# Batch 0 of a cross-attention and ELU kernel: a new written-out order, with one conversion step per weight block on GpSimd

## The chip, the cores and the metric

The kernel runs on one NeuronCore of a Trainium2 chip. The metric is the device time of one execution in microseconds (us). A core has TensorE (PE in the profile) for matmuls, VectorE (DVE), ScalarE (ACT) and GpSimd (POOL) for elementwise work, and SyncE (SP), which here only issues DMA transfers. Each engine runs its own queue of instructions in order and waits on semaphores for the others. PSUM has eight banks of 128 x 512 float32; matmuls write there.

## What is computed

The input `x` is (8 batches, 8 heads, 512 tokens, 64), `state` is (8, 8, 32, 64). For each batch and head the tokens read from the states and the states from the tokens, by softmax attention; both results are concatenated to 544 rows of 512 columns per batch and go through a feed-forward layer with an ELU:

```python
scores = scale * np.matmul(x, state.transpose(0, 1, 3, 2))
a = softmax(scores)                      # over the 32 states
xread = np.matmul(a, state)
scores2 = scale * np.matmul(state, x.transpose(0, 1, 3, 2))
a2 = softmax(scores2)                    # over the 512 tokens
sread = np.matmul(a2, x)
out = np.concatenate([xread, sread], axis=2)
x = out.transpose(0, 2, 1, 3).reshape(B * S, H * D)     # 4352 x 512
h = x @ w_in                             # 512 x 2048
g = np.where(h > 0.0, h, np.exp(np.minimum(h, 0.0)) - 1.0)
return (g @ w_out).astype(np.float32)    # 2048 x 512
```

`x` and `state` are float32. `w_in` and `w_out` arrive as float64, so that the kernel reads 8 bytes for each weight and has to make a float32 of them by integer and float operations on their low and high 32-bit words.

## The kernel before

The tokens of a batch go through the layer as 16 slices of the hidden dimension (`fo`, 128 wide each). Since `xread` is a product with the states, the kernel doesn't form it: `make_m` multiplies the states by `w_in` once per batch (a product `m` for each 512 hidden columns `c`), and `ffn1` multiplies `m` by the turned softmax weights `aT`. `exp_part` and `max_part` form the ELU into `g_all`, and a second product with `w_out` gives the output. The rows that the states read are gathered in `read` and put through the layer at the end (`states`).

Batches 1 to 7 run in `batch`: all 16 slices of `ffn1`, then the second product in a Strassen form, with the attention of the next batch hooked between its steps. x of batches 2 to 7 comes a second time as 32 x 32 blocks (`load_blocks`), which VectorE turns (`turn_blocks`); their turned softmax weights are made by VectorE and transfers (`move_state`). In batch 1 VectorE also forms the weight sums for Strassen (`weight_sum`).

Batch 0 (`first_batch`) is different: the weights are still arriving. They are cut into 32 blocks of 128 x 512 weights (16 of `w_in`, four for each `c`; 16 of `w_out`, one for each `fo`). For each block a transfer loads the 512 KB of float64 (`load_weights`, tile `raw`), ScalarE makes three passes (`convert_1`: the low word scaled and shifted to a float, the same made a whole number, the absolute value of the high word), and VectorE makes four (`convert_2`: a clamp, a shift with a mask, a join with the sign bits, and the addition of the low part, which the profile calls CUSTOM_DVE_ANT_0). A few blocks (`NRAW` = 7) are in flight; each `convert_2` is followed by `fetch`, which issues the next load. After the last block `fetch` loads batch 1's x and writes the converted `w_in` to memory (`w_in_mem`), from where later batches bring it back.

The order of all of batch 0's work, and of batch 1's attention behind it, is written out by hand as the string `plan`. Each engine executes its own instructions in exactly this order (`InOrder`). The names in it:

- `kT`/`kTc`, `kU`/`kUc`: turn the states of batch 0, of the others, on PE and copy them out; `x:b.i`/`xc:b.i`: turn half of x on PE, copy it out; `sc`: the scores.
- Softmax of head group g: `tr` (32 x 32 turn), `tm` (maximum over states), `ps` (subtract, GpSimd), `te` (exp), `su` (sum), `pm` (scale, GpSimd), `tt` (turn to `aT`); for the state side `mx` (maximum), `ae` (exp), `sd` (reciprocal of the total), `sT`/`sTc` (turn on PE, copy), `sr`/`src` (`state_read`, `keep_read`).
- `w:k.1`, `w:k.2`: the two parts of the conversion of block k.
- `M:0.c.h`, `Mc`: half of `make_m`, its copy. `M:1.0` makes batch 1's first two products.
- `F:fo` is `ffn1`, `R:fo` is `exp_part`, `E:fo` is `max_part`, `O:fo` is `ffn2_row`, which adds slice `fo` to the four output banks 0 to 3.
- `Z:n`: n matmuls of the identity, which only keep PE busy.

F needs the turned weights `tt` and an `Mc` copy, which needs converted `w_in` blocks; O needs E and one converted `w_out` block.

Of the kernel before, what the change touches and what calls it, by code (L numbers as in the profile page):

```python
# [10 lines left out]
FP32 = mybir.dt.float32  # L11
# [14 lines left out]
def kernel(  # L26
# [61 lines left out]
    def pair(i):  # L88

        return psum[:, i : i + 2]  # L90
# [39 lines left out]

    x_t, st, m_t = {}, {}, {}

    def load_x(b, engines):
        x_t[b] = xpool.tile([P, R, DM], FP32, name="x_sb")
        x_v = x[b].rearrange("h (p r) d -> p r h d", r=R)
        for r in range(R):
            engines[r % len(engines)].dma_start(
                out=x_t[b][:, r].rearrange("p (h d) -> p h d", d=D), in_=x_v[:, r]
            )

    def load_blocks(b):

# [16 lines left out]
    def turn_blocks(b, m):  # L159

        i, j = divmod(m, 2)
        if j == 0:
            st[b, "xT", i] = work.tile([P, 2, R * P], FP32, tag="w", name="xT_b")
        st[b, m] = st[b, "xT", i][:, j]
        vector.transpose(st[b, m], st[b, "blocks", i][:, j])
# [18 lines left out]
        return raw  # L184

    def turn_states(raw, b0, b1):
        ps = st["k_ps"] = pair(6)[:, :, : (b1 - b0) * 64].rearrange("p t (b q) -> p t b q", q=64)
        for b in range(b1 - b0):
            transpose(ps[:, :, b], raw[:, b].rearrange("p c d -> p (c d)"))

# [14 lines left out]
    def high_words(raw):  # L205
        return raw.bitcast(U32).rearrange("p n (j w) -> p n j w", w=2)[:, :, :, 1]

    def convert_1(dst, raw):

        lo, hi = low_words(raw), high_words(raw)

        scalar.activation(
            out=lo.bitcast(FP32), in_=lo, func=AF.Copy, scale=2.0**-29, bias=2.0**23
        )
        scalar.activation(out=lo, in_=lo.bitcast(FP32), func=AF.Copy, bias=-(2.0**23))


        scalar.activation(out=dst, in_=hi.bitcast(FP32), func=AF.Abs)  # L220

    def convert_2(dst, raw):
        lo, hi = low_words(raw), high_words(raw)
        vector.tensor_scalar(
            out=dst, in0=dst, scalar1=as_float(896 << 20),
            scalar2=as_float((1151 << 20) - 1), op0=ALU.max, op1=ALU.min,
        )

        bits = dst.bitcast(U32)
        vector.tensor_scalar(  # L230
            out=bits, in0=bits, scalar1=3, scalar2=0x3FFFFFF8,
            op0=ALU.logical_shift_left, op1=ALU.bitwise_and,
        )
        vector.scalar_tensor_tensor(
            out=bits, in0=hi, scalar=0xC0000000, in1=bits,
            op0=ALU.bitwise_and, op1=ALU.bitwise_or,
        )
        vector.tensor_tensor(out=bits, in0=bits, in1=lo, op=ALU.add)
# [18 lines left out]
                transpose(ps[:, :, j, r], x_t[b][:, r, m * P : (m + 1) * P])  # L257
        st[b, "xT", i] = ps

    def copy_x(b, i):  # L260
        xT = opool.tile([P, 2, R * P], FP32, tag="o", name="xT")
        for j in range(2):
            st[b, 2 * i + j] = xT[:, j]
            scalar.copy(
                out=xT[:, j].rearrange("p (r t q) -> p t r q", t=2, q=64),
                in_=st[b, "xT", i][:, :, j],
            )

    def by_state(b, rhs, first=6):

# [147 lines left out]
    def make_m(b, c, h=None, first=6):  # L418

        c_in = c if b < 2 else c % 2  # L420
        halves = slice(2 * c_in, 2 * c_in + 2) if h is None else slice(2 * c_in + h, 2 * c_in + h + 1)
        assert h is None or b == 0
        st[b, "m", c] = by_state(b, [w_in[:, halves, m] for m in range(NP)], first)

    def copy_m(b, c, g, copy):
        if g == 0:
            m_t[b, c] = mpool.tile([P, G, 512], FP32, name="m_sb")
        copy(out=m_t[b, c][:, g], in_=st[b, "m", c][:, g])

    def copy_half(b, c, h):  # L430
        if h == 0:
            m_t[b, c] = mpool.tile([P, G, 512], FP32, name="m_sb")
        scalar.copy(
            out=m_t[b, c][:, :, h * 256 : (h + 1) * 256], in_=st[b, "m", c][:, :, :256]
        )

    def exp_part(ps):
# [301 lines left out]
    def first_batch():  # L739
# [4 lines left out]

        plan = """
            kT kTc x:0.0 xc:0.0 x:0.1 w:0.1 xc:0.1 w:0.2 w:1.1 sc:0 Z:14 tr:0.0 tr:0.1 w:2.1 tm:0.0
            tm:0.1 ps:0.0 w:3.1 mx:0.1 mx:0.0 ps:0.1 w:1.2 ae:0.0 te:0.1 ae:0.1 sd:0.0 su:0.1 w:5.1
            M:0.0.0 sd:0.1 pm:0.1 w:3.2 Mc:0.0.0 te:0.0 sT:0 w:4.1 tt:0.1 su:0.0 sTc:0 w:5.2 pm:0.0  # L750
            w:8.1 Z:8 sr:0 tt:0.0 src:0 w:2.2 Z:14 F:0 w:6.1 F:1 w:8.2 R:0 M:0.0.1 R:1 E:0 Mc:0.0.1
            E:1 O:0 w:9.1 w:4.2 w:10.1 w:9.2 F:2 w:7.1 w:6.2 M:0.1.0 F:3 R:2 w:7.2 Mc:0.1.0 O:1
            w:11.1 E:2 R:3 w:10.2 M:0.1.1 w:12.1 F:4 w:11.2 Mc:0.1.1 O:2 R:4 E:3 w:14.1 w:12.2 F:5
            w:13.1 E:4 w:14.2 O:3 R:5 w:16.1 E:5 w:13.2 F:6 w:17.1 w:16.2 M:0.2.0 R:6 F:7 w:18.1
            w:17.2 O:4 Mc:0.2.0 w:18.2 w:20.1 kU w:15.1 E:6 O:5 w:20.2 w:21.1 w:15.2 w:19.1 F:8 kUc
            O:6 R:8 w:21.2 R:7 w:22.1 E:7 M:0.2.1 E:8 F:9 w:19.2 Mc:0.2.1 w:23.1 M:0.3.0 F:10 w:22.2
            w:24.1 O:7 w:23.2 R:9 Mc:0.3.0 E:9 w:25.1 w:24.2 M:0.3.1 F:11 Mc:0.3.1 R:10 w:25.2 O:8
            R:11 E:10 w:26.1 E:11 F:12 w:29.1 w:26.2 O:9 w:30.1 w:29.2 w:27.1 F:13 w:30.2 w:28.1
            O:10 w:27.2 R:13 R:12 w:28.2 x:1.0 w:31.1 O:11 E:12 E:13 xc:1.0 w:31.2 x:1.1 O:12 xc:1.1
            sc:1 O:13 mx:1.1 mx:1.0 ae:1.1 tr:1.0 ae:1.0 tr:1.1 sd:1.0 sT:1 tm:1.0 tm:1.1 ps:1.0  # L760
            F:14 sTc:1 sd:1.1 ps:1.1 te:1.0 sr:1 R:14 su:1.0 F:15 te:1.1 pm:1.0 E:14 src:1 su:1.1
            O:14 R:15 tt:1.0 pm:1.1 E:15 tt:1.1 M:1.0 O:15 Mc:1.0
        """.split()
        make_identity(nc, ident)
        o_ps = [bank(c) for c in range(R)]
        order = [lambda k=k: load_w_in(0, k) for k in range(4)]
        for c in range(1, FC + 1):
            if c < FC:
                order += [lambda c=c, k=k: load_w_in(c, k) for k in range(4)]
            order += [lambda fo=fo: load_w_out(fo) for fo in range(4 * c - 4, 4 * c)]  # L770
        w, h, e = [], {}, {}

        def fetch():
            if len(w) == 12 and len(raw_states) == 1:
                raw_states.append(load_states(1, B))
            if len(w) < len(order):
                w.append(order[len(w)]())
            elif 1 not in x_t:
                load_x(1, [sync])
                for c in range(FC):  # L780
                    k = slice(2 * c, 2 * c + 2)
                    sync.dma_start(out=w_in_mem[:, k], in_=w_in[:, k])

        raw_states = [load_states(0, 1, [sync, scalar])]
        load_x(0, [sync, scalar])
        for k in range(NRAW):
            fetch()
        groups = {
# [8 lines left out]
        for step in plan:  # L797
# [5 lines left out]
                copy_states(*((0, 1) if name == "kTc" else (1, B)))  # L803
            elif name == "Z":
                for i in range(num[0]):
                    matmul(bank(3)[:, :P], ident, ident, start=True, stop=True)
            elif name in groups:
                groups[name](*num)
            elif name in whole:
                whole[name](*num)  # L810
            elif name == "w":
                (convert_1, convert_2)[num[1] - 1](*w[num[0]])
                if num[1] == 2:
                    fetch()
            elif name == "F":
                h[num[0]] = ffn1(0, num[0])
            elif name == "R":
                e[num[0]] = exp_part(h[num[0]])
            elif name == "E":
                max_part(num[0], e[num[0]], h[num[0]])  # L820
            elif name == "O":
                ffn2_row(o_ps, num[0])
            elif name == "x":
                turn_x(*num)
            elif name == "M":
                make_m(*num)
                if len(num) == 2:
                    make_m(1, 1, first=4)
            elif name == "xc":
                copy_x(*num)  # L830
            else:
                assert name == "Mc", step
                if len(num) == 3:
                    copy_half(*num)
                else:
                    for g in range(G):
                        copy_m(*num, g, scalar.copy)
        for g in range(G):
            copy_m(1, 1, g, scalar.copy)

# [6 lines left out]
    def batch(b):  # L847
        if b + 1 < B:
            load_blocks(b + 1)
        for fo in range(FO):  # L850
            elu(ffn1(b, fo), fo)
            if fo > 11 and b + 1 < B:
                turn_blocks(b + 1, fo - 12)
            if fo == FO // 4 + 1:
                for c in (2, 3):
                    make_m(b, c, first=6 if c == 2 else 0)
            if FO // 4 + 1 <= fo < FO // 4 + 5:
                c, g = divmod(fo - FO // 4 - 1, G)
                copy_m(b, 2 + c, g, vector.tensor_copy)
# [50 lines left out]
                )  # L910

    first_batch()
    load_x(2, [sync])
    for e in (scalar, gpsimd):
        e.on = False
    for b in range(1, B):
# [32 lines left out]
```

## Time and profile before

| quantity | value |
|---|---|
| time, median of three runs | 747.63 us (746.75 to 747.82) |
| span of the profiled execution | 744.4 us, 11377 instructions |
| PE busy | 723.7 us (97%) |
| VectorE busy | 486.0 us (65%) |
| ScalarE busy | 293.3 us (39%) |
| GpSimd busy | 34.4 us (5%), 38 instructions |
| first F of batch 0 starts | 31.96 us |
| last O of batch 0 ends, first F of batch 1 starts | 128.7 us |
| conversion of the last weight block ends | 105.5 us |

The profile gives the time of one execution from its first to its last instruction. Busy time of PE is not PE at its peak: matmuls are pipelined and their ends are modelled, so the spacing of their starts says more than their lengths. In the views of the trace a row begins with the start and the length in us, then the engine, the line (all instructions issued through `InOrder` have line 100), the operation, the tile written and the tile read, the shapes, the count of instructions merged into the row, and in brackets how long the engine had been idle and who released it.

### The profile page before, as it was taken

To read this page: it belongs to the slowest core of one execution; us is meant where nothing else is said; L and a number is where in the kernel's file an instruction comes from. 1 tells how busy PE (TensorE), PEld (TensorE's weight loads), DVE (VectorE), ACT (ScalarE), POOL (GpSimd) and SP (SyncE) were. 2 spreads that over 40 slices of the span, in tenths; PEclk is the share of its full clock that TensorE was granted. 3 is DMA by queue.
4 is the path that set the end of the run, shared out by engine and by line. 5 is a ranking of instruction groups with operands and counts; after the bars stand their busy time and mean duration, and the time that the engine had idled before them with its cause. 6 is when DMAs were issued, how large, how long until landed. Compare 5 with 4: busy or idle time off the path is not lost.

```text
span 744.4 us, 11377 instructions
## 1 busy us (share of the span) xinstructions
PE 723.7 (97%) x4472; PEld 502.5 (68%) x4472; DVE 486.0 (65%) x892; ACT 293.3 (39%) x539; POOL 34.4 (5%) x38
## 2 busy tenths in 40 slices
PE   4899999989999999999999999999999999999998
PEld 2544444348874798469944896479746894699886
DVE  2999975799437883677556864787367845556231
ACT  5899955542126311651055203621264106400420
POOL 0100002002000200010000200020002000000000
PEclk9999999999999999999999999999999999999999
DMA  9667900801634063503461164307340403003000
GB/s 282 225 201 239 326 0 1 167 4 22 177 94 133 5 179 84 160 1 106 122 153 46 26 173 110 116 13 187 83 144 1 143 33 137 1 1 142 29 4 25
DMA packets 126366, 76.25 MB, mean 102 GB/s; under 512 B 113768, under 2 KB 114280, under 8 KB 122472
## 3 DMA queue, kind: packets, MB, share of 16 engines
q1 hardware_dynamic: 124004, 74.90, 34.8%
q10 hardware_dynamic: 2308, 0.62, 0.4%
q8 instruction: 35, 0.57, 0.3%
q14 instruction: 19, 0.16, 0.1%
HBM read 59.24 MB, written 13.11 MB: 97 GB/s over the span
## 4 chain that ended last, share of the span: by engine, by line
PE 89%; DVE 6%; SPq 1%; DMA 1%; ACT 1%; issue 1%; POOL 0%; ACTq 0%; DVEq 0%; POOLq 0%
PE ps L100 89%; DVE w_in L100 2%; SPq L100 1%; DMA x_sb<-in_x_dram 1%; DVE g_all L100 1%; DVE total_t L100 0%; DVE s L100 0%; DVE top L100 0%; DVE w_out L100 0%; ACT e_sb L100 0%; POOL t_sb L100 0%; ACT xT L100 0%; DVE xT_b L100 0%; DVE aT L100 0%; DVE t_sb L100 0%
## 5 line engine op out<-in xcount | busy, mean ns | idle before, releaser
L100 PE MATMUL ps<-w_out,g_all 128*128 128x256 f32 (+2 forms) x1088 | 232.5, 366 | 1.1 <-DVE g_all L100 0.8
L100 PE MATMUL ps<-aT,m_sb 128*128 128x512 f32 x512 | 226.3, 595 | 1.1 <-DVE m_sb L100 0.8
L100 PEld LDWEIGHTS ps<-w_out,g_all 128*128 128x128 f32 x1088 | 176.6, 191 | 53.5 <-issue 37.1
L100 PEld LDWEIGHTS ps<-aT,m_sb 128*128 128x128 f32 x512 | 95.4, 190 | 122.0 <-issue 109.1
L100 ACT ACTIVATE e_sb<-ps 128x512 f32<-128x512 f32 (+1 forms) x144 | 82.5, 573 | 220.4 <-PE ps L100 205.1
L100 DVE SCALAR_TENSOR_TENSOR g_all<-e_sb,ps 128x512 f32<-128x512 f32 (+1 forms) x144 | 94.2, 656 | 101.0 <-ACT e_sb L100 100.4
L100 DVE TENSOR_TENSOR o_sb<-o_sb,ps 128x128 f32<-128x128 f32 (+2 forms) x170 | 52.6, 310 | 75.2 <-PE ps L100 73.5
L100 ACT ACTIVATE e_sb<-e_sb 128x512 f32<-128x512 f32 (+1 forms) x144 | 87.3, 606 | 4.6
L100 PE MATMUL ps<-t_w,s 128*128 128x256 f32 (+1 forms) x480 | 88.8, 339 | 0.0
L100 PEld LDWEIGHTS ps<-t_w,s 128*128 128x128 f32 x480 | 77.6, 191 | 8.1 <-DVE o_sb L100 0.2
L100 ACT COPY o_sb<-ps 128x512 f32<-128x512 f32 (+2 forms) x52 | 20.6, 424 | 151.7 <-PE ps L100 144.6
L100 ACT ACTIVATE raw<-raw 128x512 f32<-128x512 uint32 x64 | 43.7, 683 | 1.0
L100 DVE TENSOR_TENSOR s<-s,g_all 128x512 f32<-128x512 f32 (+1 forms) x36 | 32.2, 897 | 15.9 <-PE ps L100 15.5
L100 POOL TENSOR_TENSOR t_sb<-t_sb,top_t 128x512 f32<-128x512 f32 x16 | 16.7, 1047 | 517.0 <-DVE top_t L100 517.0
L100 DVE TENSOR_TENSOR g_all<-g_all,s 128x512 f32<-128x512 f32 (+1 forms) x36 | 32.1, 891 | 9.6 <-PE ps L100 9.6
L100 PE MATMUL ps<-w_in,kT 64*32 64x512 f32 (+1 forms) x576 | 34.0, 547 | 0.9 <-ACT a_s L100 0.9
L100 DVE TENSOR_TENSOR g_all<-g_all 128x512 f32<-128x512 f32 (+1 forms) x36 | 32.2, 894 | 0.5
L100 DVE TENSOR_TENSOR s<-g_all 128x512 f32<-128x512 f32 (+1 forms) x36 | 31.6, 883 | 0.8 <-DMA aT_s<-a_blocks 0.4
L100 PE MATMUL ps<-t_w,g_all 128*128 128x128 f32 (+1 forms) x240 | 32.1, 282 | 0.0
L100 PE MATMUL ps<-w_in,s 128*128 128x128 f32 x240 | 31.2, 277 | 0.0
L100 PEld LDWEIGHTS ps<-t_w,g_all 128*128 128x128 f32 x240 | 29.8, 192 | 0.5
L100 PEld LDWEIGHTS ps<-w_in,s 128*128 128x128 f32 x240 | 28.7, 192 | 0.6 <-DVE o_sb L100 0.5
(86 smaller groups left out, 557.1 us busy)
## 6 DMA issues: line engine op xcount, KB each, us to landing
w_in<-w_in_mem SPq DMA_DIRECT2D x26, 1024.0 KB, 5.9
raw<-in_moe_w_in_dram SPq DMA_DIRECT2D x16, 512.0 KB, 4.6
raw<-in_moe_w_out_dram SPq DMA_DIRECT2D x16, 512.0 KB, 4.5
out_dram<-o_sb SPq DMA_DIRECT2D x16, 512.0 KB, 2.8
x_sb<-in_x_dram SPq DMA_DIRECT2D x30, 256.0 KB, 4.9
x_blocks<-in_x_dram SPq DMA_DIRECT2D x96, 64.0 KB, 2.4
w_in_mem<-w_in SPq DMA_DIRECT2D x4, 1024.0 KB, 8.3
aT_s<-a_blocks SPq DMA_DIRECT2D x96, 32.0 KB, 1.9
```

Source lines behind the costliest of these rows:

```text
L100: ins = getattr(self.engine, name)(*args, **kw)
```

## The change

The conversion is cut into smaller steps, and one of them goes to GpSimd for each block. For even blocks (`held`) it is the clamp (`hold`), which VectorE did; for odd blocks it is the second pass on the low word (`whole_low`), which ScalarE did. So VectorE has three passes for even blocks and four for odd ones, ScalarE three and two. In the plan `w:k.1` is ScalarE's part, `w:k.0` GpSimd's and `w:k.2` VectorE's.

The plan of batch 0 is new. x of batch 0 is loaded in two halves of the heads, and each turned half is copied by ScalarE (`xc`) and VectorE (`xd`) together. `w_out` blocks are loaded right after the four `w_in` blocks of the same `c`. Two conversions instead of five stand ahead of the first F on VectorE; the states of the other batches are turned early (`kU`); the third and fourth M are made whole. Batch 1's x is now loaded as blocks and turned by VectorE (`bt`), and its state weights are turned by `move_state` (`ab`) like those of the later batches; the read of its states moves into `batch(1)` after slice 5, with the load of batch 2's x. The save of `w_in` to memory is issued after the plan. Some PSUM banks change to fit.

```diff
-    def load_x(b, engines):
+    def load_x(b, engines, parts=1):
         x_t[b] = xpool.tile([P, R, DM], FP32, name="x_sb")
         x_v = x[b].rearrange("h (p r) d -> p r h d", r=R)
...
+        n = H // parts
+        for i in range(parts):
+            for r in range(R):
+                engines[r % len(engines)].dma_start(
+                    out=x_t[b][:, r, i * n * D : (i + 1) * n * D].rearrange(
+                        "p (h d) -> p h d", d=D
+                    ),
+                    in_=x_v[:, r, i * n : (i + 1) * n],
+                )
...
-        ps = st["k_ps"] = pair(6)[:, :, : (b1 - b0) * 64].rearrange("p t (b q) -> p t b q", q=64)
+        ps = st["k_ps"] = pair(2 if b0 else 6)[:, :, : (b1 - b0) * 64].rearrange("p t (b q) -> p t b q", q=64)
...
+    def whole_low(raw, engine):
+        lo = low_words(raw)
+        if engine is scalar:
+            scalar.activation(out=lo, in_=lo.bitcast(FP32), func=AF.Copy, bias=-(2.0**23))
+        else:
+            engine.tensor_scalar(
+                out=lo, in0=lo.bitcast(FP32), scalar1=-(2.0**23), scalar2=None, op0=ALU.add
+            )
...
+    def hold(dst, engine):
+
+        engine.tensor_scalar(
             out=dst, in0=dst, scalar1=as_float(896 << 20),
             scalar2=as_float((1151 << 20) - 1), op0=ALU.max, op1=ALU.min,
         )
...
         plan = """
...
+            kT kTc x:0.0 xc:0.0 xd:0.0 x:0.1 xd:0.1 xc:0.1 sc:0 w:0.1 tr:0.1 tr:0.0 w:1.1 w:0.0
+            tm:0.1 tm:0.0 mx:0.1 w:1.0 w:2.1 mx:0.0 w:0.2 ps:0.1 ae:0.1 w:1.2 ae:0.0 ps:0.0 te:0.1
+            Z:26 sT:0 w:2.0 te:0.0 kU sTc:0 su:0.1 M:0.0.0 w:3.1 su:0.0 pm:0.1 sr:0 kUc pm:0.0 w:4.1
+            tt:0.1 w:3.0 tt:0.0 Mc:0.0.0 w:2.2 w:5.1 Z:8 F:0 w:4.0 w:6.1 w:3.2 F:1 w:5.0 R:0 sd:0.1
+            M:0.0.1 w:4.2 w:6.0 Mc:0.0.1 w:7.1 E:0 R:1 w:7.0 w:5.2 O:0 w:8.1 E:1 w:7.2 w:10.1 w:8.0
...
+            w:27.2 w:29.1 F:11 w:30.1 w:29.0 E:10 M:0.3 w:28.2 O:10 R:11 w:30.0 w:29.2 Mc:0.3 w:31.1
+            F:12 E:11 w:31.0 w:30.2 O:11 R:12 bt:1.2 w:31.2 F:13 E:12 bt:1.1 O:12 R:13 bt:1.0 bt:1.3
+            E:13 sc:1 F:14 mx:1.0 tr:1.0 ae:1.0 mx:1.1 O:13 R:14 sd:1.0 tm:1.0 ae:1.1 E:14 ps:1.0
+            sd:1.1 ab:1 te:1.0 F:15 su:1.0 O:14 R:15 tr:1.1 pm:1.0 tm:1.1 tt:1.0 ps:1.1 E:15 te:1.1
+            M:1.0 su:1.1 pm:1.1 O:15 Mc:1.0 tt:1.1
         """.split()
+        held = range(0, 32, 2)
...
+        order = []
+        for c in range(FC):
+            order += [lambda c=c, k=k: load_w_in(c, k) for k in range(4)]
+            order += [lambda fo=fo: load_w_out(fo) for fo in range(4 * c, 4 * c + 4)]
...
             elif 1 not in x_t:
+                load_blocks(1)
                 load_x(1, [sync])
...
-        load_x(0, [sync, scalar])
+        load_x(0, [sync, scalar], 2)
...
+                if step == 0:
+                    hold(dst, gpsimd) if holds else whole_low(raw, gpsimd)
+                elif step == 1:
+                    low_part(raw)
+                    if holds:
+                        whole_low(raw, scalar)
+                    high_part(dst, raw)
+                else:
+                    if not holds:
+                        hold(dst, vector)
+                    join(dst, raw)
                     fetch()
...
+        for c in range(FC):
+            k = slice(2 * c, 2 * c + 2)
+            sync.dma_start(out=w_in_mem[:, k], in_=w_in[:, k])
...
+                if b == 1:
+                    state_read(1)
+                    keep_read(1)
+                    load_x(2, [sync])
                 for c in (2, 3):
-                    make_m(b, c, first=6 if c == 2 else 0)
+                    make_m(b, c, first=0 if (c == 2) == (b == 1) else 6)
...
     first_batch()
-    load_x(2, [sync])
```

## The prediction

> **What bounds the kernel now.** I read the page's shares first: TensorE (PE) is busy 97% of the span, so only stretches in which it stands or starts late can be won. The chain of waits says where those are. Its columns are start, length (us) and what was waited for:
>
> ```profile
> 2.37 6.56 DMA x_sb<-in_x_dram
> ...
> 31.29 0.62 DVE aT L100
> ...
> 36.40 0.61 DVE g_all L100
> 37.05 102.14 PE ps L100 x470
> ```
>
> Before 37 us the chain goes through the load of x, then VectorE (DVE), and after it through PE alone to 139 us. So the start belongs to DMA, ScalarE and VectorE. The windows view (busy us and instruction count of each engine per stretch) shows how close the others come afterwards:
>
> ```profile
> 32.00:37.00 5.00, 4.26 (x24) 1.58 (x24) 4.79 (x10) 2.50 (x5) 0.00 (x0) 1.00 0.86 290
> 37.00:60.00 23.00, 22.95 (x82) 9.80 (x83) 22.07 (x41) 21.48 (x37) 0.00 (x0) 1.00 0.65 200
> 60.00:100.00 40.00, 40.00 (x163) 16.78 (x162) 38.13 (x70) 37.61 (x64) 0.00 (x0) 1.00 0.73 242
> 100.00:128.70 28.70, 28.70 (x203) 12.67 (x202) 15.87 (x34) 13.55 (x28) 4.15 (x4) 1.00 0.00 1
> ```
>
> After the time columns stand PE, PE weight loads, VectorE, ScalarE and GpSimd. From 37 to 100 us PE is full, but VectorE is at 95% and ScalarE at 94%: the conversion of the weights only just keeps up. GpSimd does nothing there. Whatever brings PE forward must bring VectorE forward too. The timeline prices the work on PE:
>
> ```profile
> 95.89 1.88 PE L100 MATMUL ps<-aT,m_sb 128*128 128x512 f32 x4
> 97.60 3.60 PE L100 MATMUL ps<-w_out,g_all 128*128 128x512 f32 x8
> 101.13 0.71 PE L100 MATMUL ps<-ident,x_sb 64*128 64x64 f32 x16
> 101.77 3.70 PE L100 MATMUL ps<-w_out,g_all 128*128 128x512 f32 x8
> ```
>
> By the starts, an F (two matmuls of `ffn1`) after another costs 1.71 us, an O (`ffn2_row`) 3.5, half of x's turn 0.65. Batch 0's last O ends and batch 1's first F starts at 128.72.
>
> **What the Trainium skill says.** "SBUF — State Buffer", section "Who interferes with whom": VectorE and GpSimd share one pair of SBUF ports under an exclusive lock; a VectorE instruction in a two-port mode (`tensor_scalar`, copies), or with two SBUF inputs against a GpSimd instruction that reads SBUF, blocks fully until the other is done. The trace agrees:
>
> ```profile
> 28.27 1.56 DVE L100 TENSOR_SCALAR w_in<-w_in 128x512 f32<-128x512 f32 x2
> 28.50 1.05 POOL L100 TENSOR_TENSOR t_sb<-t_sb,total_t 128x512 f32<-128x512 f32 x1 [3.57 <-DVE total_t L100]
> ...
> 91.58 0.69 DVE L100 SCALAR_TENSOR_TENSOR w_out<-raw,w_out 128x512 uint32<-128x512 uint32 x1
> 92.30 0.69 DVE L100 CUSTOM_DVE_ANT_0 w_out<-raw,w_out 128x1024 uint16<-128x1024 uint16 x1
> 92.91 0.88 DVE L100 TENSOR_SCALAR w_out<-w_out 128x512 f32<-128x512 f32 x2
> 93.83 0.69 DVE L100 SCALAR_TENSOR_TENSOR w_out<-raw,w_out 128x512 uint32<-128x512 uint32 x1
> ...
> 176.62 1.05 POOL L100 TENSOR_TENSOR t_sb<-t_sb,total_t 128x512 f32<-128x512 f32 x1 [1.69 <-DVE total_t L100]
> 176.98 1.24 DVE L100 TENSOR_TENSOR t<-t_w,t 128x512 f32<-128x512 f32 x1
> ```
>
> Two `tensor_scalar` take 0.88 us alone (92.91) and 1.56 when GpSimd runs at 28.50. The two-input instruction at 176.98 takes 1.24 where its like in batch 1 takes 0.68: GpSimd ends at 177.67, and it ends 0.55 later. So a blocked instruction is shortened by about 0.13 [...], and one GpSimd instruction of length p put between two such VectorE ones costs VectorE p - 0.13. All instructions of a conversion on VectorE are of these two kinds; only `max_part`, which reads PSUM and one SBUF tile, and some of the softmax are free of it.
>
> **The start.** x comes in halves of four transfers. They landed at 5.9, 7.1, 8.3 and 8.9 us by PE's starts; the first half, half of the bytes, should be there by 6.4. Its turn (0.8) and its two copies, now one each on ScalarE and VectorE at 0.55 rather than two in a row, lie beside the second half's landing. That lands at about 9 (more issues, same bytes); turn 0.9, copies 0.6: scores at 10.65 instead of 13.72. VectorE starts on them 2.1 later (15.84 before): 12.8. Then two `tr` 1.3, two `tm` 1.25, two `mx` 1.55: 16.9. Then only two conversions stand ahead of the first F, not five: 1.81 (blocks whose clamp is on GpSimd: one block's 2.25, from the starts 91.58 and 93.83, less 0.44) and 2.25, with 0.5 lost to GpSimd: 21.5. Sums 1.8, the other states' copy 1.1, two turns 1.3: first F at 25.8 instead of 31.96, so 6.2 earlier. The loads of the other states now come ahead of raw block 4; ScalarE is not there before 20, so I cost it nothing.
>
> **What PE needs from there.** 16 F and 16 O: 16 x (1.72 + 3.43) = 82.4; M: one half 0.6, two halves 1.2, two whole 1.95; scores 1.1; batch 1's first M 1.95: 89.2 in all, so 115.0 if nothing stands in its way. Gone are x's turn (1.4) and the turn of batch 1's weights (1.0), whose work goes to VectorE and transfers; the read of batch 1's states (1.1) moves into batch 1; the turn of the states (0.65) now lies in the start.
>
> **What VectorE needs.** After the first F, 30 blocks are left: 15 x 1.81 + 15 x 2.25 = 60.9. Twelve `max_part` at 0.60: 7.2; two small totals and the first turn of batch 1's blocks: 1.15. Sum 69.2, so the last conversion would end at 95.0 without GpSimd. After it come E:12 (0.6) and then PE's remainder, whose order leaves no second gap: four O, two F, scores and M, 20.2. End is the last conversion + 20.8: 115.8, level with PE's bound.
>
> To this comes the lock. GpSimd has about 28 instructions in the stretch. No row shows a one-input instruction on it at this size. Upper bound: its two-input row at 28.50, 1.05 us. Lower: "GPSIMD Engine Reference", section 3.1, gives 1.03 cycles an element for at most two operations, an estimate of 0.44 us for 512 at 1.2 GHz; the same section measures 0.77 for 512 elements in a longer loop. Its section 7 has a penalty for steps above 8 bytes; the low words lie exactly 8 apart, so I take none. No run here shows any of these. I take 0.50, nearer the low end because both steps have one input and one or two operations. Cost: 28 x (0.50 - 0.13) = 10.4. `max_part` and the small work make up 12% of VectorE's time, and a waiting GpSimd instruction slips into them; I say a quarter is hidden: 7.8. The last conversion ends at 102.8, the batch at 123.6, against 128.7: 5.1 won.
>
> ScalarE isn't the bound: three instructions for 15 blocks at 1.87, two for 14 at 1.25, R at 1.2 and the copies of M are about 64 us in these 77. What waits behind a late join on VectorE is the next E, and behind that an O on PE; that is the sum's assumption.
>
> **Batch 1.** It gains 1.1 on PE and 0.5 on ScalarE. In the chain, VectorE carries the work from 140.5 to 146.3 and from 157 to 166.2, with PE standing 0.8 and 2.3 us ahead of those ends. So most of the 1.1 hides; I add 0.5. The save of `w_in` (4 MB, 8.3 us to landing each) now goes right before batch 0's stores and the x blocks of batch 2. Those blocks were issued by 148.2 and first turned at 156.3, so some 5 us of delay are hidden. Later batches are untouched. Together 747.6 - 5.1 + 0.5 = **743.0**.
>
> **Rivals.** (1) GpSimd's work slips almost wholly into gaps of VectorE: PE's 115.0 sets the end, 13.7 won, 0.5 given back: 734.4. For it: ScalarE and GpSimd steps are placed some slots ahead of each join. Against it: VectorE has few gaps. (2) GpSimd is slow, and the lock becomes the bound. At 0.77 the lock costs 28 x 0.64 x 0.75 = 13.4, the batch ends at 129.2, 748.6 in all; at 1.05, 28 x 0.92 x 0.75 = 19.3, it ends at 135.1, and the time is 754.5: slower. With nothing hidden, 761. For it: VectorE was already 95% busy, so each wait lands on the path. Against it: one input, not two. (3) The start is won but batch 1 gives it back, since VectorE bounds it and the late transfers meet it: about 747.
>
> **Chances.** Forecast 0.45 (0.40 of it faster, the rest near nothing or beyond, since p decides), hidden 0.15, slow GpSimd 0.30, given back 0.10 (0.04 faster, 0.04 same, 0.02 slower). Faster 0.59, same 0.07, slower 0.34. The range goes from the hidden case to a little beyond the slow one, leaving out the unhidden 761: 734 to 757.
>
> **What would show it.** First `ps<-aT,m_sb` near 26 us; scores near 10.7; GpSimd rows of 0.5 us for `raw` and `w_in`/`w_out`; VectorE's 0.69 us rows in the conversion lengthened on average, by 5 to 10 us in the stretch; last conversion near 103; batch 1's first F near 123.6. A GpSimd row of 0.8 or more, or PE waiting long on VectorE between 40 and 100 us, would make it wrong on the slow side; lengths that stay at 0.69 on the fast side.

## The result, and the profile after

The changed kernel takes 754.93 us (median of 4 runs, 754.59 to 756.5), the kernel before in the same comparison 747.73: a ratio of 1.0103, 95% interval 1.0085 to 1.012. It is slower by 7.2 us, where 743.0 and a gain were forecast. The span of the profiled execution grew from 744.4 to 752.9 us, by 8.5.

The chain of waits of the changed kernel, to be held against the one before (start, length, what was waited for):

```profile
26.85 0.65 DVE aT L100
...
30.67 1.05 DVE w_in L100
...
110.53 0.69 DVE g_all L100
111.27 35.86 PE ps L100 x212
```

VectorE is now on the chain until 111 us, where before PE carried it from 37 us. The first F did start earlier (27.65 instead of 31.96 us), but the lead was then lost. The windows of the changed kernel (after the time columns PE, PE weight loads, VectorE, ScalarE, GpSimd, then the granted PE clock, the DMA share and GB/s) show the new bound:

```profile
27.00:60.00 33.00, 29.29 (x102) 11.90 (x103) 31.08 (x52) 23.08 (x42) 24.22 (x13) 0.90 0.61 199
60.00:111.00 51.00, 46.79 (x131) 18.42 (x129) 47.93 (x76) 34.39 (x59) 29.65 (x17) 1.00 0.51 124
111.00:132.00 21.00, 20.73 (x89) 8.38 (x90) 13.17 (x29) 8.57 (x18) 4.19 (x4) 1.00 0.14 23
```

PE, full before from 37 to 100 us, now has holes; VectorE is busy 94% of 27 to 111 us. ScalarE has been relieved (from 94% of 37 to 100 us before to 68% here), which won no time. GpSimd works 53.9 us of these 84. Its groups (count, then busy us and mean ns of one, then idle time) give the price that the prediction had to guess:

```profile
L100 POOL TENSOR_SCALAR raw<-raw 128x512 uint32<-128x512 f32 x16 | 26.9, 1687 | 4.6 <-ACT raw L100 3.7
L100 POOL TENSOR_SCALAR w_in<-w_in 128x512 f32<-128x512 f32 x8 | 17.2, 2157 | 18.1 <-ACT w_in L100 16.1 <-DVE w_in L100 1.3 <-DMA raw<-in_moe_w_in_dram 0.6
L100 POOL TENSOR_SCALAR w_out<-w_out 128x512 f32<-128x512 f32 x8 | 15.9, 1988 | 11.5 <-ACT w_out L100 11.2
```

A low-word pass takes 1.69 us and a clamp 2.0 to 2.2, not 0.50. A clamp takes VectorE 0.42. How the two engines meet is seen in the timeline of the changed kernel:

```profile
47.65 1.96 POOL L100 TENSOR_SCALAR w_out<-w_out 128x512 f32<-128x512 f32 x1 [3.91 <-ACT w_out L100]
47.85 0.96 DVE L100 CUSTOM_DVE_ANT_0 w_in<-raw,w_in 128x1024 uint16<-128x1024 uint16 x1
48.73 0.41 DVE L100 TENSOR_SCALAR w_in<-w_in 128x512 uint32<-128x512 uint32 x1
49.18 0.69 DVE L100 SCALAR_TENSOR_TENSOR w_in<-raw,w_in 128x512 uint32<-128x512 uint32 x1
49.68 1.69 POOL L100 TENSOR_SCALAR raw<-raw 128x512 uint32<-128x512 f32 x1
49.90 1.09 DVE L100 CUSTOM_DVE_ANT_0 w_in<-raw,w_in 128x1024 uint16<-128x1024 uint16 x1
```

While the clamp runs from 47.65 to 49.61, one VectorE instruction is lengthened (0.96 instead of 0.69) and the next two keep their usual 0.41 and 0.69, though both are of the kinds that were expected to wait. Then the low-word pass adds 0.40 to the next one (1.09). So GpSimd's instructions are much longer than assumed, but take only a part of their length from VectorE.

VectorE's row of work from 27.43 us to the end of the last conversion at 109.16 has no gap over 0.14 us: 81.7 us for 30 blocks. By the rates of before it is 69.2 as predicted, and 0.6 for one weight sum that got in between: 11.9 are lost, 0.42 for each of 28 GpSimd instructions.

A second loss lies in batch 1. From its first F to the start of the last part of batch 2's scores pass 40.3 us (131.83 to 172.12) instead of 37.5 (128.72 to 166.23). VectorE's timeline says why; first the kernel before, from the third turn of batch 2's blocks to the fourth:

```profile
160.28 0.70 DVE L100 STREAM_TRANSPOSE xT_b<-x_blocks 128x512 f32<-128x512 f32 x1
...
164.87 0.68 DVE L100 TENSOR_TENSOR t<-t_w,t 128x512 f32<-128x512 f32 x1
165.47 0.70 DVE L100 STREAM_TRANSPOSE xT_b<-x_blocks 128x512 f32<-128x512 f32 x1
```

Then the changed kernel, up to the third turn:

```profile
163.76 0.68 DVE L100 TENSOR_TENSOR t<-t_w,t 128x512 f32<-128x512 f32 x1
...
165.49 0.69 DVE L100 TENSOR_TENSOR t<-t_w,t 128x512 f32<-128x512 f32 x1
166.09 0.69 DVE L100 TENSOR_TENSOR t_w<-t_w 128x512 f32<-128x512 f32 x1
166.70 0.69 DVE L100 TENSOR_TENSOR w_out<-w_out 128x512 f32<-128x512 f32 x1
167.30 0.68 DVE L100 TENSOR_TENSOR w_in<-w_out 128x512 f32<-128x512 f32 x1
167.90 0.70 DVE L100 STREAM_TRANSPOSE xT_b<-x_blocks 128x512 f32<-128x512 f32 x1
```

Five weight sums for the second level of Strassen (`second[k].weights`) stand ahead of the last two turns of batch 2's blocks; in the kernel before there was one between them. No line of the diff moves them. They are issued after `vector.on = False`, where the compiler of the program may choose the place, and with another order in front of them it chose another one. Three more such sums stand in batch 0, two of them right behind the last conversion and ahead of E:12; these stood there in the kernel before too (at 105.48 and 106.21 us), and the forecast left them out. PE waits 1.28 and 2.41 us for the turns; its granted clock falls to 0.82 from 172 to 180 us, and the last scores and the first M products there, 2.7 us long before (166.23 to 168.93), take 4.0 (172.12 to 176.15).

Three parts of the 8.5 us between the two spans are thus placed: 3.1 at the end of batch 0 (131.83 against 128.72), 2.8 in batch 1 and 1.3 behind it. The last 1.3 arise in the later batches. Batch 3, from first F to first F, lasts 80.8 instead of 79.7 us; it lasts 80.5 to 81.0 in every trace of the new order below and 79.7 to 79.8 in every one of the old. The cause of this stays open.

### The profile page after: what moved, and what is told of

It is laid out like the page before. It is cut to its first block, busy times and chain, and to the rows that moved or that the text cites. A ratio compares the mean times of both kernels' runs of the same rounds, so it can differ in the third digit from the quotient of the medians.

```text
span 752.9 us, 11333 instructions
## 1 busy us (share of the span) xinstructions
PE 728.7 (97%) x4396; PEld 501.0 (67%) x4396; DVE 494.5 (66%) x884; ACT 278.7 (37%) x515; POOL 94.3 (13%) x70
## 4 chain that ended last, share of the span: by engine, by line
PE 78%; DVE 13%; DMA 3%; SPq 2%; issue 2%; ACT 1%; POOL 0%; DVEq 0%; POOLq 0%
PE ps L100 78%; DVE w_in L100 4%; DVE w_out L100 4%; SPq L100 2%; DVE g_all L100 1%; DMA raw<-in_moe_w_in_dram 1%; DVE s L100 1%; DMA x_sb<-in_x_dram 1%; DMA aT_s<-a_blocks 1%; ACT e_sb L100 0%; DMA s_first<-in_state_dram 0%; DVE m_sb L100 0%; DVE total_t L100 0%; DVE top L100 0%; DVE xT_b L100 0%
## 5 line engine op out<-in xcount | busy, mean ns | idle before, releaser
L100 PE MATMUL ps<-w_out,g_all 128*128 128x256 f32 (+2 forms) x1088 | 236.1, 369 | 6.1 <-DVE g_all L100 2.5
L100 PEld LDWEIGHTS ps<-w_out,g_all 128*128 128x128 f32 x1088 | 177.3, 192 | 63.7 <-issue 36.8
L100 DVE SCALAR_TENSOR_TENSOR g_all<-e_sb,ps 128x512 f32<-128x512 f32 (+1 forms) x144 | 94.3, 655 | 100.7 <-ACT e_sb L100 100.2
L100 PE MATMUL ps<-w_in,kT 64*32 64x512 f32 (+1 forms) x544 | 36.4, 587 | 3.7 <-DVE w_in L100 3.0
L100 ACT ACTIVATE raw<-raw 128x512 f32<-128x512 uint32 (+1 forms) x48 | 32.5, 677 | 0.5
```

The source lines that it names most:

```text
L100: ins = getattr(self.engine, name)(*args, **kw)
```

## Experiments

Theory A: GpSimd's steps cost VectorE more through the shared ports than they take off it. Theory B: the new order itself lost the time, by its start, by PE's clock or in batch 1. Theory C, for batch 1: the sums that moved ahead; its rival D: the late transfers. The table gives the time of each run, the ratio to the kernel before in the same comparison, and from its profile the start of the first F, the end of the last conversion, the start of batch 1's first F, and the us from there to the start of the last part of batch 2's scores.

| run | time | ratio (95%) | first F | last conversion | batch 1's F | batch 1 |
|---|---|---|---|---|---|---|
| before | 747.7 | | 31.96 | 105.5 | 128.7 | 37.5 |
| changed | 754.9 | 1.0103 (1.0085 to 1.012) | 27.65 | 109.2 | 131.8 | 40.3 |
| e1_no_gpsimd | 747.2 | 0.9989 (0.9981 to 0.9997) | 26.16 | 102.3 | 123.5 | 40.3 |
| e2_clamp_only | 747.2 | 0.9992 (0.9982 to 1.0001) | 26.09 | 100.8 | 123.5 | 40.3 |
| e3_weights_after_turns | 750.0 | 1.0029 (1.002 to 1.0038) | 27.81 | 107.8 | 129.2 | 37.4 |
| e4_before_spare_clamp | 757.8 | 1.0123 (1.0101 to 1.0144) | 34.36 | 116.3 | 139.6 | 37.5 |
| e5_no_gpsimd_late | 743.8 | 0.9939 (0.9924 to 0.9954) | 26.64 | 102.3 | 123.5 | 37.4 |
| e6_clamp_only_late | 742.1 | 0.9916 (0.9901 to 0.9931) | 26.61 | 100.7 | 122.4 | 37.4 |
| e7_before_late | 746.6 | 0.9975 (0.9965 to 0.9986) | 32.23 | 105.7 | 129.0 | 36.2 |
| e8_low_only | 756.5 | 1.0105 (1.009 to 1.012) | 26.34 | 111.8 | 133.0 | 40.3 |
| e9_before_spare_low | 761.8 | 1.0198 (1.0178 to 1.0218) | 33.82 | 118.7 | 142.1 | 37.5 |
| e10_before_spare_low_dense | 759.4 | 1.0165 (1.0146 to 1.0184) | 34.88 | 117.4 | 140.6 | 37.5 |
| e11_x_whole | 743.2 | 0.9947 (0.9931 to 0.9964) | 27.47 | 101.9 | 123.3 | 37.4 |
| e12_all_clamps_late | 742.5 | 0.9942 (0.9925 to 0.996) | 28.07 | 101.1 | 123.2 | 37.4 |

### No GpSimd step, and only one kind of it

```diff
-                if step == 0:
-                    hold(dst, gpsimd) if holds else whole_low(raw, gpsimd)
-                elif step == 1:
+                if step == 1:
                     low_part(raw)
-                    if holds:
-                        whole_low(raw, scalar)
+                    whole_low(raw, scalar)
                     high_part(dst, raw)
-                else:
-                    if not holds:
-                        hold(dst, vector)
+                elif step == 2:
+                    hold(dst, vector)
                     join(dst, raw)
```

> The changed kernel with no conversion step on GpSimd: the clamp of even blocks back on VectorE (ahead of the join), the low word's second pass of odd blocks back on ScalarE; order otherwise that of the change. Theory A (GpSimd's steps of 1.6 to 2 us cost VectorE more through the shared ports than the clamps they take off it): in the profile of the changed kernel VectorE needs 81.8 us from 27.4 to 109.2 for work that is 69.9 at the rates of before, 11.9 lost to some 28 GpSimd steps, 0.42 each; the 15 clamps that come back cost 15 x 0.44 = 6.6. So the last conversion should end some 5 us earlier, near 104, batch 1's first F near 126, and the time be about 749. Theory B (the new order itself, not GpSimd, is what lost: PE's slow clock from 33 to 42 us, the start, batch 1): VectorE and ScalarE only get more to do, and the time is 755 to 762.

Measured: 747.2 us, and batch 1's first F 8.3 us earlier than in the changed kernel. VectorE has 15 clamps more in the stretch and is done 6.9 us sooner. That is more than the 749 and the 126 of the expectation. Theory A holds, and for batch 0 B falls: the new order without GpSimd gains 5.2 us up to the end of batch 0. Batch 1 and what lies behind it take nearly all of it back, so for batch 1 B stands; the runs with late sums below take it up.

e2 keeps the clamps of even blocks on GpSimd, e8 the low-word passes of odd blocks:

```diff
                 if step == 0:
-                    hold(dst, gpsimd) if holds else whole_low(raw, gpsimd)
+                    if holds:                          # e2
+                        hold(dst, gpsimd)
...
+                    if not holds:                      # e8
+                        whole_low(raw, gpsimd)
```

> The changed kernel with only the clamps of even blocks on GpSimd (16 instructions of 1.95 us); the low word's second pass of odd blocks is back on ScalarE. Theory A: half of the lost 11.9 us goes, VectorE's own work stays as in the changed kernel: last conversion near 103, time about 749, the same as with no GpSimd step, since a clamp costs 0.42 through the ports and saves 0.44. If the longer clamp costs more than the low-word pass, it is slower than the run with no GpSimd step, 751 or more. Theory B: ScalarE only gets more to do, time 755 or more.

> The changed kernel with only the low word's second pass of odd blocks on GpSimd, the clamps all on VectorE. By differences, 16 clamps on GpSimd changed nothing (first F of batch 1 at 123.5 with and without), so the 16 low-word passes must carry the 8.3 us, about 0.5 each though they are the shorter ones (1.65 against 1.95 us). Expected: first F of batch 1 at 131 to 132, time 754 to 756. If the two kinds only hurt together (GpSimd's queue too full), 748 to 750.

Measured: with the clamps 747.2 us, where 749 was expected, and batch 1's first F at 123.5 as without GpSimd. That these agree is in part chance: VectorE's last conversion ends 1.5 us sooner with the clamps on GpSimd, but two weight sums (1.3 us) follow it there, which in e1 stand further back. With the low-word passes 756.5, first F at 133.0, some 1 us beyond what was expected. The summed length of VectorE's conversion instructions tells the two kinds apart: it is 71.4 us without GpSimd, 69.4 with 16 clamps there, 78.6 with 16 low-word passes. A clamp saves VectorE 0.42 and gives back (69.4 - 71.4 + 16 x 0.42) / 16 = 0.29 of it; a low-word pass saves VectorE nothing and costs (78.6 - 71.4) / 16 = 0.45. It was taken off ScalarE, which had time. So e2 and e8 part what A had put into one price: the low-word passes are the loss, the clamps are not.

### The ports alone

The kernel before gets one GpSimd instruction per block on a spare tile that nobody reads: e4 a clamp, e9 the low-word pass at steps of 8 bytes, e10 the same on adjacent elements.

```diff
                 (convert_1, convert_2)[num[1] - 1](*w[num[0]])
+                if num[1] == 1:
+                    gpsimd.tensor_scalar(
+                        out=spare, in0=spare, scalar1=as_float(896 << 20),
+                        scalar2=as_float((1151 << 20) - 1), op0=ALU.max, op1=ALU.min,
+                    )
```

> The kernel before, with one extra GpSimd clamp of 128 x 512 on a spare tile for each of the 32 blocks, placed after ScalarE's part in the order; nothing reads the tile, so no engine waits for it and only the shared ports can cost time. Theory A (0.42 us of VectorE for each): VectorE, 95% busy in batch 0, needs 32 x 0.42 = 13 us more, and the time is 755 to 760. If a GpSimd step held the ports for all of its 1.95 us: 50 us more, 785 or above. If the cost in the changed kernel is the chain (joins that wait for the slow GpSimd step) and not the ports: 747 to 749.

> The kernel before with one extra GpSimd low-word pass (float read and uint32 written, both at steps of 8 bytes, 512 elements) on a spare tile for each of the 32 blocks; nothing reads it. If the ports alone make the low-word pass dear (0.5 to 0.6 us of VectorE each by the difference of the runs with and without it), VectorE loses 16 to 19 us and the time is 762 to 767, clearly above the 757.8 of the spare clamps. If in the changed kernel it was the chain (VectorE's clamp and join waiting for a slow pass), the spare pass costs no more than the spare clamp: 756 to 759.

> As the run before, but the spare pass reads and writes 512 adjacent elements. If the 8-byte steps make the pass hold the ports longer, this costs clearly less than the strided one, as much as a spare clamp or less: 755 to 759. If the kind of operation does (one operand, float to uint32), it costs the same as the strided one.

The groups of GpSimd in e4, e9 and e10, one fence for each:

```profile
L100 POOL TENSOR_SCALAR t<-t 128x512 f32<-128x512 f32 x32 | 63.7, 1990 | 2.3
```

```profile
L100 POOL TENSOR_SCALAR t<-t 128x512 uint32<-128x512 f32 x32 | 53.5, 1671 | 2.3
```

```profile
L100 POOL TENSOR_SCALAR t<-t 128x512 uint32<-128x512 f32 x32 | 50.3, 1572 | 2.3
```

The lengths of 2.0, 1.7 and 1.6 us are those of the instructions themselves. In the spare runs no data connects them to the rest. Only their place in GpSimd's queue does: the second `ps` comes at 20.76 instead of 18.81 us in e4, and VectorE doesn't wait for it. VectorE's conversions sum to 72.8 us in the kernel before, 83.1 in e4, 86.9 in e9 and 84.9 in e10: 0.32, 0.44 and 0.38 us for each GpSimd instruction. The times rise by 9.2, 14.8 and 12.3 us (ratio times 747.7). So GpSimd's steps lengthen VectorE's instructions without any wait on data. That the shared ports do it fits which instructions are lengthened: `max_part`, which the prediction counts as free of the lock, ran beside a clamp seven times in e4 and took 0.67 to 0.68 us, as before. The strided pass fell just short of the expected 762 to 767 but is clearly dearer than the clamp, though it is shorter. The dense one came out between the two: by these sums the steps cost 0.06 and the kind of operation another 0.06, from one trace each; neither of the two pure answers held.

In e4 GpSimd ran 26 clamps in one piece:

```profile
31.20 53.65 POOL L100 TENSOR_SCALAR t<-t 128x512 f32<-128x512 f32 x26
```

If each had kept VectorE out for all of its length, VectorE could have converted next to nothing between 31 and 85 us. It converted on, with one in every few instructions lengthened. The trace shows which: of VectorE's 128 conversion instructions 49 met no GpSimd instruction, and none of these was lengthened. Of the 24 that began at least 1.0 us after a GpSimd instruction had started, and were over at the latest 0.15 us after the start of the next, none was either. Of the other 55, 36 were. So a clamp holds VectorE up around its start, not through its second half.

### Batch 1's weight sums

```diff
-            hooks += [lambda: second[4].weights(t_w[4]), lambda: second[3].weights(b22)]
-            hooks += [lambda: second[5].weights(t_w[1]), lambda: second[7].weights(t_w[3])]
+            def late(i, b):
+                vector.on = True
+                second[i].weights(b)
+                vector.on = False
+
+            hooks += [lambda: late(4, t_w[4]), lambda: late(3, b22)]
+            hooks += [lambda: late(5, t_w[1]), lambda: late(7, t_w[3])]
```

> The changed kernel, but the second-level weight sums of batch 1 (second[k].weights) keep their place in VectorE's program order, behind the turns of batch 2's blocks and the softmax of batch 2, and can't be moved ahead. Theory C (of the 5.9 us by which batch 2's scores end late, 2.8 arise in batch 1, because five such sums of 0.6 us now stand ahead of the last two turns on VectorE): PE's first scores of batch 2 complete some 3 us earlier against batch 1's start, PE's clock doesn't drop there, three sums of 0.6 also leave batch 0: time 749 to 751. Rival D (the late loads of the blocks, behind the save of w_in, are the cause): the turns wait all the same, 754 to 755.

> The kernel before with batch 1's second-level weight sums kept behind the turns in the same way. Theory C says that the loss in batch 1 came from the changed order alone: in the kernel before only one such sum stands ahead of the last turn, so this should win at most 0.6 us in batch 1, and nothing in batch 0, where PE was the bound by 105 us: 746.5 to 748. If it wins 4 us here as well, the gain is not an undoing of the change but a gain of its own.

Measured in the changed kernel: 750.0 us, batch 1 37.4 us long as before the change, and 2.6 us less in batch 0. In e3's timeline of PE the wait for the last turn is 1.84 us, no longer than in the kernel before (2.32):

```profile
163.71 1.08 PE L100 MATMUL ps<-xT_b,kT 64*32 64x512 f32 x12
166.63 0.62 PE L100 MATMUL ps<-xT_b,kT 64*32 64x512 f32 x2 [1.84 <-DVE xT_b L100]
```

All transfers are as in the changed kernel, so D falls: neither the late blocks nor the late save of `w_in` cost anything that can be seen. PE's clock doesn't fall here either: the fall at the start of batch 2 is in all four traces of the new order with free sums (changed, e1, e2, e8) and in none of the five with late ones.

In the kernel before the same pin (e7) wins 1.7 us (0.9975, 0.9965 to 0.9986), 1.3 of them in batch 1. That is more than the 0.6 expected: the pin is in part a gain of its own. So the kernels are compared fairly with the pin in both, and then batch 1 is 1.2 us longer in the new order (37.4 in e3, 36.2 in e7). The read of batch 1's states, which the change moved here, takes 1.03 us of PE in e3 and isn't hidden:

```profile
139.62 1.10 PE L100 MATMUL ps<-x_sb,aT_s 128*32 128x64 f32 x64
140.65 1.95 PE L100 MATMUL ps<-w_in,kT 64*32 64x512 f32 x32
```

### Put together, and the smaller parts

> Both undoings together: no conversion step on GpSimd, and batch 1's second-level weight sums kept behind the turns. If the two losses are separate they add: without the GpSimd steps batch 1's first F came 8.3 us earlier than in the changed kernel, and with the sums kept back batch 1 lasted 37.4 instead of 40.3 us. Expected: first F of batch 1 at 121 to 123.5, batch 2's scores 37.4 later, time 742 to 743.5. If the sums' 2.6 us in batch 0 and the lock share a cause, 745.

> As the run before, but with the clamps of even blocks on GpSimd. Theory A: a clamp through the ports costs VectorE about what it saves it (0.34 against 0.42 by the sums of the two runs without late sums), so it is within 1 us of the version with no GpSimd step: 741.5 to 743.5.

e5 (no GpSimd step) takes 743.8 us, e6 (clamps only) 742.1, both with the sums kept late. The two losses add, to within 0.3 us of the range expected for e5. e6 beats both kernels: 0.9916 of the kernel before. Its windows show PE near full again and VectorE as busy as before, but for an earlier start:

```profile
26.00:60.00 34.00, 29.51 (x109) 12.03 (x110) 32.35 (x58) 31.71 (x56) 15.14 (x8) 1.00 0.73 231
60.00:100.00 40.00, 39.88 (x120) 16.64 (x119) 38.30 (x65) 35.48 (x60) 13.22 (x7) 1.00 0.60 141
100.00:122.00 22.00, 22.00 (x93) 8.69 (x92) 14.37 (x30) 8.58 (x17) 4.19 (x4) 1.00 0.12 20
```

Between e5 and e6 the intervals overlap, though each of e6's four runs is below each of e5's; the profiles put 1.1 us between their ends of batch 0.

Two variations of e6, `load_x(0, [sync, scalar])` without halves (e11) and `held = range(32)` (e12):

> The version with only clamps on GpSimd and late sums (742.1 us), with x of batch 0 loaded in four whole transfers again. The halves let the scores start at 9.4 us [...] and end at 12.8. Whole: x lands near 8.9, second half turned by 9.8, scores 11 to 13. If the halves matter, the first F comes 0.5 to 1.5 us later and the time is 742.6 to 743.6; if VectorE's later work sets the start of F anyway, 742.1 within 0.3.

> The version with only clamps on GpSimd and late sums, with all 32 clamps on GpSimd instead of 16. By the sums each clamp saves VectorE 0.42 and costs 0.34 through the ports: 16 more win about 1 us if GpSimd (64 us of work in some 85) keeps up: 740.5 to 742. If its queue becomes the bound, joins wait for it: 744 or more.

Without the halves the first F and batch 1's first F both come 0.86 us later, and the time is 743.2; that is the size expected, but the intervals of the two runs touch. With all clamps on GpSimd (742.5 us) the first F is 1.5 us later, since two slow clamps instead of one stand ahead of the softmax steps on GpSimd, and 0.7 are won back in the stretch: no gain, where up to 1.6 was expected. The clock of PE, which falls to 0.74 between 30 and 40 us in the changed kernel, was not tried by itself: VectorE's row is unbroken there, and e2, with 0.83 in the same ten us, has batch 1's first F where e1, with 1.00, has it.

## Why the prediction was wrong

**The direction was wrong, by the price of GpSimd's steps and by batch 1.** Batch 0 ends 8.2 us later than forecast: VectorE's row begins 1.6 later, GpSimd's steps take 4.1 more of it, one weight sum in it takes 0.6, and from the last conversion to the end it is 1.9 more. The range (734 to 757) held the time, through the rival that named the cause: a slow GpSimd, the lock as the bound, 754.5. But that rival came out right by luck, since its p (the length of a GpSimd step) was 1.05 and its lock was whole.

- The start: scores at 10.65, first F at 25.8. Measured 9.43 and 27.65. The scores began earlier but took 3.4 us (the same 16 matmuls take 1.09 at 114.90; why they were slow isn't shown), so VectorE started on them at 12.90, as predicted (12.8), which is luck in part. The miss is in the two conversions ahead of F: 5.8 us (16.86 to 22.66) instead of 4.6, by GpSimd; without GpSimd F is at 26.16. Before the change four conversions, not five, were done ahead of F; the fifth began beside it.
- The step "I take 0.50" failed. The instructions measured 1.57 to 1.99 us in the spare runs, where they wait for no data. The Trainium skill's "GPSIMD Engine Reference", section 3.1, with its 1.03 cycles an element for up to two operations, doesn't fit them: 1.99 us at the page's 1.2 GHz is 4.7 cycles an element (an estimate that spreads the whole length over 512 elements). The choice was made towards the low end, below the 0.77 us of the same section, because one operand looked cheap; the upper bound taken from a two-operand row (1.05) was not a bound.
- The step "28 x (0.50 - 0.13), a quarter hidden: 7.8" measured 11.9. The rule behind it, that a blocked instruction waits for the whole of the other, was read from two `tensor_tensor` rows, which themselves show losses of 0.68 and 0.56 for a step of 1.05 us, and doesn't hold for these steps: at p = 1.8 it would give 28 x 1.67 = 47 us. Two wrong terms, p too small and the hold too long, worked against each other: 0.28 us for a step by the sum, 0.42 measured. The size that counted was not asked for at all: the cost per kind, 0.3 for a clamp against 0.42 saved, 0.45 for a low-word pass against nothing saved on VectorE (by the runs e1, e2 and e8).
- That was the error of reasoning: the prediction counted half of GpSimd's steps as relief although those 16 relieved ScalarE, which its own sum (64 us of 77) showed to have time. A price through a shared port should have been set against what the bound engine saves, kind by kind.
- "End is the last conversion + 20.8": measured 22.7, since two weight sums (1.3 us) stand in between, as they did before the change. In the five runs where these are kept late it is 21.2 to 22.1.
- Batch 1, "+0.5": measured 2.8, and 1.3 more behind it by PE's clock. Of the parts named, the transfers were rightly called hidden; the read of the states was not, it shows as some 1.0 us once the sums are pinned in both kernels. What failed most was that the sum had no term for anything else: an order left free moved. "Later batches are untouched" failed too, by 1.3 us in the two traces.
- Right: PE's need, near enough (e6 ends batch 0 at 122.4 from a first F at 26.6, some 6 above the bound of 89.2; that sum took 3.43 for an O where its own rows give 3.5, 1 us in all), ScalarE not the bound, no wait of VectorE on data, and the last conversion near 103 in the versions without low-word passes (100.7 to 102.3).

## What to carry to other kernels

Work may go to GpSimd only if the engine that is the bound gets rid of more than the shared ports take from it, so weigh each kind of step by itself: here a clamp was about even or a little ahead, and a step taken from an engine with time to spare was a plain loss. When an order in front of a free-floating piece of work changes, look at where that work lands; compare the order of instructions, not only the diff, and pin what must not pass a critical instruction.

## What the runs showed of the hardware

A GpSimd `tensor_scalar` of 128 x 512 took 1.99 us with two operations (e4) and 1.57 with one and a conversion to uint32 (e10), longer than its `tensor_tensor` with two inputs (1.05 us in the kernel before). The Trainium skill's "SBUF — State Buffer", section "Who interferes with whom", has the shared ports held for the whole instruction; here 32 such clamps, 63.7 us of GpSimd, lengthened VectorE's instructions by 10.2 us in all. The measurement decides: the hold is a part of the instruction, 0.32 us of 1.99 on average, and 0.44 of 1.67 for the strided pass. For the clamps of e4 it lies around the start of the instruction, as shown above. In the changed kernel the picture is less clean: of 23 conversion instructions that began 1.0 us or more after the start of a GpSimd step and were over before the next took hold, 4 were lengthened, and in e8, with low-word passes alone, 6 of 11. Where a low-word pass holds the ports stays open.

The low-word passes cost more than these lengths. Against e2 the changed kernel ends its last conversion 8.3 us later: its first F is 1.6 late, VectorE's instructions behind it are 5.2 longer in sum, and the gaps between them 1.5. The gaps lie ahead of the additions: 22 of these 30 begin 0.14 us after the instruction before them has ended instead of 0.03; in e2 it is 7, and in e1, and in e4, where nothing reads what GpSimd wrote, it is none. What they wait for stays open.
